# Block-sparse attention with a gated feed-forward: the first batch's attention over all keys with a per-key bias, the other three sparse, loads and groups reordered

## The chip, the cores and the metric

The kernel runs on one core of one Trainium2 chip. Five engines work from queues of their own, each in the order in which the program gave it its instructions: TensorE (PE in the profile, with its weight loads as PEld), VectorE (DVE), ScalarE (ACT), GpSimd (POOL) and SyncE (SP). SP only starts transfers here, POOL starts transfers and computes, and 16 DMA engines carry all transfers. The metric is the device time of one execution in microseconds (us); lower is better.

## The reference

There are 4 batches, 8 heads, 768 positions, head size 64. The positions form 24 blocks of 32. A query block meets its own block and the two beside it, the first and the last block, and three sampled blocks; the first and the last query block meet all keys. Behind it stand a root-mean-square norm and a gated feed-forward of width 1536 (FFN below), in float32 with bfloat16 inside the kernel.

```python
scores = scale * np.matmul(q, k.transpose(0, 1, 3, 2))
mask = np.abs(blk_i - blk_j) <= window
mask = mask | (blk_i == 0) | (blk_j == 0) | (blk_i == n_blocks - 1) | (blk_j == n_blocks - 1)
for qb in range(n_blocks):
    for kb in sampled_blocks[qb]:
        mask[qb * block:(qb + 1) * block, kb * block:(kb + 1) * block] = True
scores = np.where(mask, scores, -1000000000.0)
attn = np.exp(scores - np.max(scores, axis=-1, keepdims=True))
attn = attn / (np.sum(attn, axis=-1, keepdims=True) + 1e-09)
x = np.matmul(attn, v).transpose(0, 2, 1, 3).reshape(B * S, H * D)
xn = x / np.sqrt(np.mean(x * x, axis=-1, keepdims=True) + 1e-06) * rms_g
g = xn @ w_gate
out = (g * (1.0 / (1.0 + np.exp(-g))) * (xn @ w_val)) @ w_out
```

## The kernel before, in words

**Chunks and steps.** A chunk is 128 queries, four query blocks, of one batch. Each batch has six: five of neighbouring blocks, and one "wide" chunk of the blocks 0, 23, 1, 22 (chunks 5, 11, 17 and 22 of the 24). The outer loop (L581) has a step for each chunk and one more; a step has 10 positions, step 6 has 20. The loop only sets the order in which instructions are given to the queues: jobs are attached to a position by `do(n, ...)`, and after each position `position()` adds pieces of FFN work (L506).

**Attention of chunk i.** The keys that each query block meets are gathered into `kg`: DVE copies the neighbouring blocks and the first and last (`gather_k`, L298, L302), ACT or POOL copies the sampled ones, one block and sample at a time, at an address from a register (`sampled_k`, L310). `by_act` (L225) says which engine: ACT for two samples of three, and for all three in the first two chunks of each batch. The registers are filled from the table `kofs` (L185) by loads on ACT or POOL (`addresses`, L235). DVE copies the queries into `Qd` (`gather_q`, L325, L327). `scores` (L355) makes tiles of 8 products 128x64, 4 tiles in a sparse chunk and 8 in a wide one, and ACT takes the exponential of each tile into `ex` (L361). Two tiles `st` have room in PSUM. The values are fetched row by row: `table` (L261) writes the batch's values as bfloat16 to the DRAM tile `vtab`, and POOL starts an indirect transfer for each query block (`gather_v`, L335) with the row numbers `vidx` (L193 to L218). Step i+1 begins with `values(i)` (L376), 64 products 128x66 (128 in a wide chunk), and DVE divides by the sums into `stage` (L397, L398). Then come the squares on ACT (L405), the power on POOL (L409, L410), the product `xs` on DVE, and the turn of `xs` into `xg`: by PE (L430) for chunks 0 to 3 and the last group, by a DMA transpose started by SP (L424) for the others.

**FFN.** Chunks form groups, `sizes = [2, 2, 2, 3, 4, 4, 4, 3]`. A group's pieces are 12 gate and 12 value pieces (L445, L456: four products each, 128 columns per chunk; tanh on ACT at L449, two products on DVE at L460 and L464) and then four down pieces per chunk (L474, three products 128x512 each). `entry` (L560) gives the position from which a group's pieces are laid in, evenly until the next group's entry: in steps 3, 5, 6 (position 10), 10, 14, 18 and 22. The last group stands alone at the end. All FFN tiles and transposes share four PSUM tiles (`ps_f`).

**Before the loop.** SP loads the values of batch 0 (`load_v`), POOL the keys and 32 of each 128 query rows (`load_turned`, which also casts), PE turns the keys and those queries (`turn`, `turn_first_queries`), DVE and ACT copy them out. `keep_busy` is products that nobody reads. Weights are loaded by POOL, half of them from `W_AT` in steps 0 to 2. Batch 1 is loaded in steps 3 and 4, and batches 2 and 3 in the first four steps of the batch before them (POOL for keys and queries, SP for values). `gains` (L543) loads the norm's gain through SP, and DVE scales it, in step 3.

**Queues.** POOL's transfers use eight completion semaphores in turn, so each waits until the eighth before it has landed.

Of the kernel before, what the change touches and what calls it, by code (L numbers as in the profile page):

```python
# [18 lines left out]
def kernel(  # L19
# [18 lines left out]
    P = 128  # L38
# [36 lines left out]
    sizes = [2, 2, 2, 3, 4, 4, 4, 3]  # L75
# [64 lines left out]
    vtab = [dram.tile([NT + HB, 2 * HV], BF16, name=f"vtab{i}") for i in range(B)]  # L140

    NS = NRND * HB
    samp_i = const.tile([NS, NB * NRND * 2], I32, name="samp_i")
# [11 lines left out]
    def iota(t, lo, hi, cols, step, base):  # L155
        nc.gpsimd.iota(t[lo:hi, cols], pattern=[[step, cols.stop - cols.start]], base=base,
                       channel_multiplier=1)

    p_i = const.tile([NS, 1], I32, name="p_i")
    qb_i = const.tile([NS, NB], I32, name="qb_i")  # L160
    vidx = const.tile([P, NB], I32, name="vidx")
    every = slice(0, NB)
    nc.gpsimd.iota(p_i, pattern=[[0, 1]], base=0, channel_multiplier=1)
    nc.gpsimd.iota(qb_i, pattern=[[1, NB]], base=0, channel_multiplier=0)
    for pr in range(NP):
        load_turned(0, pr, 0)
    ident32 = const.tile([P, P], FP32, name="ident32")
    make_identity(nc, ident32)
    iota(vidx, F0 - HB, W0, every, 0, -HB)
# [5 lines left out]
    for pr in range(NP):  # L175
        load_turned(0, pr, 1, (0, QR))
    idle = const.tile([P, 2 * HV], BF16, name="idle")
    nc.vector.memset(idle, 0.0)
    for i in range(2):
        nc.vector.memset(Qd[i], 0.0)  # L180
    for i in range(2):
        nc.vector.memset(Vs[i][:, :, :, D:VW], 1.0)
    samp = samp_i.rearrange("p (a r w) -> p a r w", r=NRND, w=2)[:, :, :, 0]
    kofs = const.tile([1, NB * NRND], I32, name="kofs")
    nc.vector.tensor_scalar(out=kofs.rearrange("p (r a) -> p a r", r=NRND), in0=samp[0:1],  # L185
                            scalar1=float(HB), scalar2=None, op0=ALU.mult)
    ident = const.tile([P, P], BF16, name="ident")
    nc.vector.tensor_copy(out=ident, in_=ident32)
    qb = const.tile([NS, NB], FP32, name="qb")
    nc.vector.tensor_copy(out=qb, in_=qb_i)  # L190
    pp_i = const.tile([NS, 1], I32, name="pp_i")
    pp = const.tile([NS, 1], FP32, name="pp")
    nc.vector.tensor_scalar(out=pp_i, in0=p_i, scalar1=HB - 1, scalar2=None, op0=ALU.bitwise_and)  # L193
    nc.vector.tensor_scalar(out=pp, in0=pp_i, scalar1=float(NT), scalar2=None, op0=ALU.add)
    rb = const.tile([NS, NB, NRND], FP32, name="rb")
    good = const.tile([NS, NB, NRND], FP32, name="good")
    tmp = const.tile([NS, NB, NRND], FP32, name="tmp")
    nc.vector.tensor_copy(out=rb, in_=samp)

    nc.vector.tensor_tensor(out=tmp, in0=rb, in1=qb.unsqueeze(2).to_broadcast([NS, NB, NRND]),  # L200
                            op=ALU.subtract)
    nc.vector.tensor_tensor(out=tmp, in0=tmp, in1=tmp, op=ALU.mult)
    nc.vector.tensor_scalar(out=good, in0=tmp, scalar1=1.5, scalar2=None, op0=ALU.is_ge)
    nc.vector.scalar_tensor_tensor(out=tmp, in0=rb, scalar=1.0 - NB, in1=rb, op0=ALU.add,
                                   op1=ALU.mult)
    nc.vector.scalar_tensor_tensor(out=good, in0=tmp, scalar=-0.5, in1=good, op0=ALU.is_le,
                                   op1=ALU.mult)
    for step in range(1, NRND):
        n = NRND - step
        nc.vector.tensor_tensor(out=tmp[:, :, 0:n], in0=rb[:, :, step:], in1=rb[:, :, 0:n],  # L210
                                op=ALU.not_equal)
        nc.vector.tensor_tensor(out=good[:, :, step:], in0=good[:, :, step:], in1=tmp[:, :, 0:n],
                                op=ALU.mult)
    nc.vector.scalar_tensor_tensor(out=tmp, in0=rb, scalar=-float(NB), in1=good, op0=ALU.add,
                                   op1=ALU.mult)
    for r, lo, hi in ((1, 0, 2 * HB), (0, 0, HB), (2, 2 * HB, 3 * HB)):
        nc.vector.tensor_scalar(out=vidx[lo:hi], in0=tmp[lo:hi, :, r], scalar1=float(HB),
                                scalar2=pp[lo:hi], op0=ALU.mult, op1=ALU.add)  # L218
# [6 lines left out]
    def by_act(c, r):  # L225
        return r + 1 < NRND or c in chunks[0][1] or c in chunks[1][1]
# [15 lines left out]
    addresses(0, ET.Activation)  # L242
    addresses(1, ET.Activation)
# [3 lines left out]

    zero_rows(0)
    mhalf = const.tile([P, 1], FP32, name="mhalf")
    nc.vector.memset(mhalf, -0.5)  # L250
    eps = const.tile([P, 1], FP32, name="eps")
    nc.vector.memset(eps, DM * 1e-6)
    gain = const.tile([P, DM], FP32, name="gain")
    rmsg = const.tile([P, NP], FP32, name="rmsg")
# [6 lines left out]
    def table(b):  # L261
        if b:
            zero_rows(b)
# [13 lines left out]
    def turn_first_queries(copy):  # L277
# [246 lines left out]
    for pr in range(NP):  # L524
        cast_v(0, pr, dve)
# [168 lines left out]
```

## Time and profile before

| | us |
|---|---|
| median of 3 runs | 358.10 (353.57, 358.10, 360.46) |
| profiled execution | 354.41, of which span 352.6 |
| busy in the span: PE, DVE, ACT, POOL | 285.6, 208.1, 193.0, 156.3 |
| first scores (L355) of chunk 0 start | 18.22 |
| `stage` (L398) of chunk 0 and chunk 5 starts | 27.54, 95.41 |
| `values` of chunks 0 to 4 follow at (DVE L397 or PE L376) | 25.9, 37.6, 43.9, 60.4, 81.1 |
| POOL: 88 indirect transfers (L335), 998 ns each | 87.8 |
| ACT: 112 exponentials (L361), 606 ns each | 65.8 |
| ACT: 208 sampled key copies (L310) | 55.4 |

The start of DVE's reciprocal (L397) marks the end of a chunk's attention. From chunk 5 on these are at 95.1, 114.5, 123.6, 137.3, 145.7, 162.5 (chunk 10), 174.1, 182.8, 195.8, 210.4, 224.2 (chunk 15), 234.3, 246.0, 256.9, 267.5, 276.3 (chunk 20), 284.6, 301.9 and 316.4. In the timeline an entry such as "x8" merges instructions of one form that follow one another; the time is that of all of them, and the bracket behind it is the idle time before it and what ended it. The ends of products are modelled, so the distance from start to start tells more of PE's pace than the length.

### The profile page before, as it was taken

Reading aid. Unit: us, or ns where it says so; the run is one execution under the profiler, and the core shown is the slowest. Engines: PE = TensorE matmul, PEld = TensorE weight load, DVE = VectorE, ACT = ScalarE, POOL = GpSimd, SP = SyncE. Lnnn points to the kernel's source line nnn. Section 1 sums busy time; section 2 is a strip of 40 time slices with the busy share of each in tenths; the row PEclk is TensorE's granted clock in tenths of the full one; section 3 lists DMA queues with packets and bytes.
Section 4 is the critical chain, followed back from the end, with each engine's and each line's share of the span. In section 5 each row is a group of like instructions: output and inputs, shape, how many; then the busy total and the mean of one; then the engine's idle time right before and its main releaser. Section 6 shows DMA issues by size and latency. Waiting matters only on the chain.

```text
span 352.6 us, 10122 instructions
## 1 busy us (share of the span) xinstructions
PE 285.6 (81%) x4021; PEld 175.6 (50%) x4021; DVE 208.1 (59%) x483; ACT 193.0 (55%) x519; POOL 156.3 (44%) x250
## 2 busy tenths in 40 slices
PE   4734777388899758578978697989999998989995
PEld 1423566256766546245645453545455554534653
DVE  7615674444756746348763487860999456661770
ACT  0563752236379764646676557656866665513422
POOL 7188895170075584713288437333654550000000
PEclk9966588679999988969998999999999999999999
DMA  7779999997379397892579996767434661002002
GB/s 213 177 174 246 189 218 215 292 207 196 112 144 273 99 225 165 150 265 53 136 137 244 220 148 146 183 132 229 115 94 105 159 187 54 3 2 89 33 0 89
DMA packets 38903, 53.94 MB, mean 153 GB/s; under 512 B 12372, under 2 KB 29576, under 8 KB 38856
## 3 DMA queue, kind: packets, MB, share of 16 engines
q0 software_dynamic: 20544, 34.81, 45.9%
q1 hardware_dynamic: 18248, 18.46, 18.7%
q8 instruction: 31, 0.51, 0.6%
q10 hardware_dynamic: 64, 0.03, 0.2%
q14 instruction: 16, 0.13, 0.1%
HBM read 52.39 MB, written 9.67 MB: 176 GB/s over the span
## 4 chain that ended last, share of the span: by engine, by line
PE 46%; DMA 13%; POOL 11%; DVE 10%; issue 9%; ACT 8%; SPq 1%; POOLq 1%; ACTq 0%; DVEq 0%
PE yp L474 14%; PE gp L445 11%; PE vp L456 11%; POOL vg L335 6%; DMA kbf<-in_k_dram 4%; PE op L376 3%; DMA vraw<-in_v_dram 3%; PE st L355 3%; ACT ex L361 3%; DMA gain<-in_moe_rms_g_dram 3%; DVE u L460 3%; PE tqk L272 2%; DMA rmsr<-in_moe_rms_g_dram 2%; DVE stage L398 2%; ACT th L449 2%
## 5 line engine op out<-in xcount | busy, mean ns | idle before, releaser
L335 POOL DMA_INDIRECT vg<-vtab,vidx x88 | 87.8, 998 | 39.5 <-issue 19.1
L445 PE MATMUL gp<-xg,wg 128*128 128x256 bf16 (+2 forms) x384 | 82.7, 341 | 8.2 <-DVE u L460 6.2
L456 PE MATMUL vp<-xg,wv 128*128 128x256 bf16 (+2 forms) x384 | 82.9, 341 | 4.1 <-DVE u L460 2.8
L361 ACT ACTIVATE ex<-st 128x512 bf16<-128x512 f32 x112 | 65.8, 606 | 9.3 <-PE st L355 9.0
L449 ACT ACTIVATE th<-gp 128x256 bf16<-128x256 f32 (+2 forms) x96 | 47.7, 497 | 42.2 <-PE gp L445 40.9
L460 DVE SCALAR_TENSOR_TENSOR u<-th,gp 128x256 bf16<-128x256 bf16 (+2 forms) x96 | 53.1, 553 | 29.2 <-ACT th L449 27.7
L474 PE MATMUL yp<-wo,hps 128*128 128x512 bf16 (+1 forms) x300 | 68.2, 375 | 0.0
L464 DVE TENSOR_TENSOR hps<-u,vp 128x256 bf16<-128x256 bf16 (+2 forms) x96 | 53.3, 555 | 11.4 <-PE vp L456 1.4
L310 ACT COPY kg<-KT 128x128 bf16 x208 | 55.4, 313 | 3.1 <-issue 3.1
L409 POOL TENSOR_TENSOR ssq<-ssq,eps 128x1 f32<-128x1 f32 x24 | 4.8, 200 | 106.4 <-ACT junk L405 100.9
L445 PEld LDWEIGHTS <-wg 128*128 128x128 bf16 x384 | 36.4, 103 | 29.8 <-issue 9.6
L456 PEld LDWEIGHTS <-wv 128*128 128x128 bf16 x384 | 37.1, 103 | 27.2 <-issue 4.1
L355 PE MATMUL st<-Qd,kg 128*128 128x64 bf16 x704 | 43.8, 203 | 8.2 <-ACT ex L361 4.3
L355 PEld LDWEIGHTS <-kg 128*128 128x128 bf16 x704 | 36.8, 105 | 24.2 <-issue 9.6
L405 ACT ACTIVATE junk<-stage 128x512 bf16<-128x512 bf16 x24 | 15.1, 630 | 52.6 <-DVE stage L398 52.6
L474 PEld LDWEIGHTS <-hps 128*128 128x128 bf16 x300 | 28.0, 99 | 26.9 <-issue 0.6
L397 DVE RECIPROCAL rz<-op 128x8 f32<-128x8 f32 x24 | 4.9, 206 | 43.8 <-PE op L376 43.8
L480 ACT ACTIVATE yo<-yp 128x512 f32<-128x512 f32 (+1 forms) x25 | 14.5, 582 | 25.7 <-PE yp L474 22.9
L325 DVE COPY Qd<-QN 64x512 bf16<-64x512 bf16 x80 | 24.5, 306 | 1.2 <-ACT QN L274 0.2
L376 PEld LDWEIGHTS <-ex 128*32 128x32 bf16 x1792 | 18.9, 98 | 12.3 <-issue 12.0
L376 PE MATMUL op<-vg,ex 128*32 128x66 bf16 x1408 | 21.5, 202 | 3.8 <-DMA vg<-vtab,vidx 3.7
L258 DVE CAST Vs<-vraw 128x768 bf16<-128x768 f32 x16 | 8.8, 566 | 22.8 <-DMA vraw<-in_v_dram 22.8
(68 smaller groups left out, 243.9 us busy)
## 6 DMA issues: line engine op xcount, KB each, us to landing
vraw<-in_v_dram SPq DMA_DIRECT2D x16, 384.0 KB, 5.9
out_dram<-yo SPq DMA_DIRECT2D x19, 256.0 KB, 3.9
vtab<-Vs SPq DMA_DIRECT2D x4, 792.0 KB, 4.0
kbf<-in_k_dram POOLq DMA_DIRECT2D x16, 192.0 KB, 6.9
qbf<-in_q_dram POOLq DMA_DIRECT2D x12, 192.0 KB, 6.7
wo<-in_moe_w_out_dram POOLq DMA_DIRECT2D x2, 768.0 KB, 18.9
vg<-vtab,vidx POOLq DMA_INDIRECT x88, 4.2
out_dram<-yo SPq DMA_DIRECT2D x16, 64.0 KB, 2.6
```

Source lines behind the costliest of these rows:

```text
L310: copy(out=kgs[i % 2][:, :, j, R0 + r * HB:R0 + (r + 1) * HB], in_=KT[b % 2][:, :, bass.ds(kat[(qbs[j], r)], HB)])
L325: copy(out=to, in_=rows[:, :, qbs[0] * HB:(qbs[0] + QB) * HB])
L335: nc.gpsimd.indirect_dma_start(vgs[i % 3][:, j, :], None, vtab[b][:], bass.IndirectOffsetOnAxis(ap=vidx[:, qbs[j]:qbs[j] + 1], axis=0))
L355: nc.tensor.matmul(out=st[:, at:at + UN], lhsT=lhsT, rhs=Qd[i % 2][:, h, :, :, j * HB:(j + 1) * HB].rearrange("p a w s -> p (a w) s"), sta ...
L361: nc.scalar.activation(out=ex.rearrange("p (u s w) -> p u s w", s=HB, w=2), in_=st.rearrange("p (u w s) -> p u s w", s=HB, w=2), func=AF.E ...
L376: nc.tensor.matmul(out=op[j * BLK:(j + 1) * BLK, h // 4, at:at + VW], lhsT=lhsT, rhs=rhs, start=(n == 0), stop=(n == of - 1))
L445: nc.tensor.matmul(out=gp[:, 0:tg], lhsT=wg[:, c, f * P:(f + 1) * P], rhs=xg[:, c, 0:tg], start=(c == 0), stop=(c == KD - 1))
L449: nc.scalar.activation(out=th[:, 0:tg], in_=gp[:, 0:tg], func=AF.Tanh, scale=0.5)
L456: nc.tensor.matmul(out=vp[:, 0:tg], lhsT=wv[:, c, f * P:(f + 1) * P], rhs=xg[:, c, 0:tg], start=(c == 0), stop=(c == KD - 1))
L460: nc.vector.scalar_tensor_tensor(out=u[:, 0:tg], in0=th[:, 0:tg], scalar=1.0, in1=gp[:, 0:tg], op0=ALU.add, op1=ALU.mult)
L464: nc.vector.tensor_tensor(out=hps[f][:, 0:tg], in0=u[:, 0:tg], in1=vp[:, 0:tg], op=ALU.mult)
L474: nc.tensor.matmul(out=yp, lhsT=hps[f][:, tt * P:(tt + 1) * P], rhs=wo[:, f, lo:hi], start=(f == 0), stop=(f == NF - 1))
```

## The change

Batch 0's attention no longer selects keys. Each tile of scores holds all 8 heads for one query block and 128 keys (every third of half the positions; `all_scores`, 12 tiles a chunk), and the exponential adds a bias for each key (a partition) from the table `hide`: 0 where the query block meets the key's block, -30000 elsewhere. `all_values` multiplies with the values as they stand in SBUF, in three parts of 64 products. Batch 0 has no `vtab`, no indirect transfers, no `kg` and no sampled copies. `hide` is made by DVE ahead of `kofs`. Steps 0 to 5 have 12 positions, a tile in each; the squares of batch 0 are taken by DVE. Chunks 2 and 3 turn `xs` by DMA. In the batches 1 to 3 `by_act` leaves every third sample to POOL. Batch 0's values are loaded by POOL behind keys and queries, `samp_i` and the gain by SP; batch 1's loads stay in steps 3 and 4. The groups become `[2, 2, 2, 4, 4, 4, 4, 2]`, entering at step 2 (position 8), 4 (10), 6 (10), 11, 15, 19 and 23.

```diff
-    sizes = [2, 2, 2, 3, 4, 4, 4, 3]
+    sizes = [2, 2, 2, 4, 4, 4, 4, 2]
...
-        nc.sync.dma_start(
+        (nc.sync if b else nc.gpsimd).dma_start(
             out=t, in_=v[b, 2 * pr:2 * pr + 2].rearrange("e (p c) d -> p e c d", p=P))
...
-    nc.scalar.dma_start(out=samp_i, in_=s32.to_broadcast([NS, NB * NRND * 2]))
-    for pr in range(NP):
-        load_v(0, pr)
+    nc.sync.dma_start(out=samp_i, in_=s32.to_broadcast([P, NB * NRND * 2]))
...
+    for pr in range(NP):
+        load_turned(0, pr, 1, (0, 2 * QR))
...
     for pr in range(NP):
-        load_turned(0, pr, 1, (0, QR))
+        load_v(0, pr)
...
+    nc.vector.tensor_tensor(out=hide, in0=keys(kb), in1=queries(qb), op=ALU.subtract)
+    nc.vector.tensor_tensor(out=hide, in0=hide, in1=hide, op=ALU.mult)
+    nc.vector.scalar_tensor_tensor(out=hide, in0=hide, scalar=1.5, in1=keys(inner), op0=ALU.is_ge,
+                                   op1=ALU.mult)
...
+    for r in range(NRND):
+        nc.vector.tensor_tensor(out=far, in0=keys(kb), in1=queries(rb[:, :, r]), op=ALU.not_equal)
+        nc.vector.tensor_tensor(out=hide, in0=hide, in1=far, op=ALU.mult)
     nc.vector.tensor_scalar(out=kofs.rearrange("p (r a) -> p a r", r=NRND), in0=samp[0:1],
                             scalar1=float(HB), scalar2=None, op0=ALU.mult)
...
-        return r + 1 < NRND or c in chunks[0][1] or c in chunks[1][1]
+        return r + 1 < NRND
...
-    addresses(0, ET.Activation)
-    addresses(1, ET.Activation)
+    for i in range(PB):
+        addresses(i, ET.Pool)
+    for i in range(2):
+        addresses(i, ET.Activation)
...
+    def all_scores(i, cc, j):
+        st = ps_s.tile([P, H, UN], FP32, name="st", tag="st")
+        for h in range(H):
+            nc.tensor.matmul(
+                out=st[:, h, :], lhsT=KT[0][:, h, cc::HC],
+                rhs=Qd[i % 2][:, h, :, :, j * HB:(j + 1) * HB].rearrange("p a w s -> p (a w) s"),
+                start=True, stop=True)
+        c = chunks[i][1][j]
+        ex = exs[(i, cc, j)] = work.tile([P, 512], BF16, name="ex", tag="ex", bufs=10)
+        nc.scalar.activation(
+            out=ex.rearrange("p (u s w) -> p u s w", s=HB, w=2),
+            in_=st.rearrange("p h (u w s) -> p (h u) s w", s=HB, w=2), func=AF.Exp, scale=SCALE,
+            bias=hide[:, cc, c:c + 1])
+    def all_values(i, cc):
+        if cc == 0:
+            ops[i] = ps_o.tile([P, 2, 512], FP32, name="op", tag="op")
+        for h in range(H):
+            at = (h % 4) * VW
+            for w in range(2):
+                for j in range(QB):
+                    ex = exs[(i, cc, j)].rearrange("p (h w s) -> p h w s", h=H, w=2)
+                    nc.tensor.matmul(
+                        out=ops[i][j * BLK:(j + 1) * BLK, h // 4, at:at + VW], lhsT=ex[:, h, w, :],
+                        rhs=Vs[0][:, 2 * cc + w, h, :], start=(h % 4 == cc + w == 0),
+                        stop=(h % 4 == 3 and cc == HC - 1 and w == 1))
...
+            nc.vector.tensor_tensor_reduce(
+                out=junk, in0=stages[i], in1=stages[i], scale=1.0, scalar=0.0, op0=ALU.mult,
+                op1=ALU.add, accum_out=ssqs[i])
...
-        if i >= 4 and i not in groups[-1]:
+        if i >= 2 and i not in groups[-1]:
...
+        if m[-1] < PB:
+            step, pos = m[-1] + 1, 8 + 2 * (m[0] > 0)
...
+            for cc in range(HC):
+                for j in range(QB):
+                    do(cc * QB + j, lambda cc=cc, j=j: all_scores(i, cc, j))
+            do(7, lambda: all_values(i, 0))
+            do(11, lambda: all_values(i, 1))
...
+            if i + 2 < PB:
+                do(10, lambda: addresses(i + 2, ET.Activation))
```

The last part of a chunk's values, `all_values(i - 1, 2)`, stands at position 1 of the next step, before that position's tile.

More of the change, by code (lines that the diff above doesn't have):

```diff
@@ L197 @@
     tmp = const.tile([NS, NB, NRND], FP32, name="tmp")
[L198 to L215, printed above, removed]
@@ L359, in scores @@
                 at += UN
-        ex = exs[(i, part)] = work.tile([P, 512], BF16, name="ex", tag="ex", bufs=9)
+        ex = exs[(i, part)] = work.tile([P, 512], BF16, name="ex", tag="ex", bufs=10)
         nc.scalar.activation(
```

213 lines of the change are left out of this document (125 added, 88 removed).

## The prediction

> **What bounds the kernel now.** I read the windows of the stages first: start, batch 0 (to chunk 5's `stage`), steps 6 to 10, 11 to 14, 15 to 18, 19 to 22, and the rest. Columns: length, busy us of PE, PEld, DVE, ACT, POOL, PE's granted clock, DMA share, GB/s.
>
> ```profile
> 0.00:18.20 18.20, 10.49 (x69) 5.17 (x70) 12.73 (x41) 5.06 (x12) 8.31 (x24) 1.00 0.75 189
> 18.20:95.00 76.80, 52.30 (x896) 39.08 (x895) 39.62 (x101) 36.10 (x107) 43.64 (x65) 0.76 0.95 209
> 95.00:162.50 67.50, 52.58 (x803) 36.84 (x795) 38.58 (x101) 44.83 (x123) 36.77 (x55) 0.90 0.76 179
> 162.50:210.40 47.90, 39.68 (x643) 23.57 (x640) 30.42 (x68) 31.14 (x87) 27.32 (x42) 0.96 0.78 163
> 210.40:256.90 46.50, 42.20 (x650) 23.40 (x649) 30.90 (x69) 31.26 (x84) 20.53 (x30) 1.00 0.65 162
> 256.90:301.90 45.00, 42.77 (x639) 22.84 (x638) 30.75 (x65) 27.95 (x74) 18.24 (x31) 1.00 0.42 112
> 301.90:352.60 50.70, 45.59 (x340) 24.71 (x338) 25.09 (x44) 16.60 (x33) 1.49 (x4) 1.00 0.12 38
> ```
>
> Batch 0 takes 77 us in which no engine is busy for more than 52; the DMA share is 0.95 and PE's clock 0.76. From step 15 on PE sets the pace. The chain of waits names what batch 0 waits for (start, length, what):
>
> ```profile
> 16.57 1.17 POOL vg L335
> ...
> 20.58 5.30 DMA vg<-vtab,vidx
> ...
> 55.73 10.32 DMA gain<-in_moe_rms_g_dram
> ```
>
> The tile view of `kofs` and the timeline of ACT show what comes before ACT's first copy:
>
> ```profile
> L235 ACTq TENSOR_LOAD <-kofs x16: 275/906/1107, 4.6 to 57.5; - x16
> ...
> 10.70 1.28 ACT L274 ACT_TABLE_LOAD   x1 [10.70 <-DVE rmsg L523]
> 11.99 0.80 ACT L274 COPY KT<-tqk 128x768 bf16<-128x768 bf16 x1
> ```
>
> Six register loads begin at 4.6, when `kofs` is there, and the table load follows at 10.70: 1.01 us each. The timeline also gives the price of a tile, on a fast and on a slow PE:
>
> ```profile
> 83.81 1.07 ACT L361 ACTIVATE ex<-st 128x512 bf16<-128x512 f32 x2
> ...
> 67.70 0.63 PE L355 MATMUL st<-Qd,kg 128*128 128x64 bf16 x8
> 68.14 1.04 PE L456 MATMUL vp<-xg,wv 128*128 128x256 bf16 x4
> ```
>
> Two exponentials with nothing between end 1.07 after the first began, so the second began 0.47 after it. Eight score products take 0.44 here (67.70 to 68.14); at full clock 0.23 (two such sets, 82.19 to 82.42 to 82.66).
>
> **The change, part by part.** The profiled run (354.4) is the second fastest of four executions whose mean is 356.6; I add differences in the span to that mean.
>
> *What goes.* 22 indirect transfers (POOL 22 x 1.3 with their gaps, 29 us; 22 x 270 KB, from the tile's shape, 5.9 MB) and `vtab` (0.8 MB), of 16.1 MB moved at 209 GB/s in 76.8 us; 52 sampled copies on ACT (0.266 each, 13.8 us), 14 on POOL, the DVE copies for `kg`. The gain's wait goes too: its load stood in SP's queue behind value loads that wait for DVE, now nothing is ahead of it, and PE's 4.6 us of idleness at 66.9 with it. So batch 0 is no longer held by transfers; next is the trio PE, ACT, DVE.
>
> *Start: later by 3.7.* `kofs` is now made after the 3x24 table: DVE has the identity at 5.16+0.26 as before, then some 23 small operations at the 0.15 to 0.25 of their kind, 4.4 us, so `kofs` ends at 9.85 instead of 4.6. ACT waits for it: four loads, 4.1, and the table load, 1.28, put its first copy at 15.3 instead of 11.99. Behind that copy stand PE's third and fourth key turn (PSUM tiles), the queries, `Qd` and the first scores: 6.2 us in the profile, and up to 1.7 more if PE, idle for over 4 us by then, is at half clock (six turns take 0.82 instead of 0.49). 21.5 to 23.2; I take 21.9. The earlier keys gain nothing, ACT isn't there to copy them. POOL has seven such loads, 6.7 us; the second half of the queries and the first weights queue behind them to about 22 to 25. That costs nothing while chunk 0's first third (to about 30) covers it, up to 5 us else.
>
> *Steps 0 to 2: 32.4.* A dense chunk has 12 tiles and 192 value products. With two PSUM tiles a pair costs an exponential (0.60), eight products and their latency (0.39), two semaphores: 1.07, 0.54 a tile (exponentials at 85.03 and 86.12 had this); at half clock 1.34, 0.67. Each third of the values is 0.63 at full clock (64 products, 113.92 to 114.55), 1.2 at half (37.59 to 38.79), 0.4 and 0.9 of which ACT can't cover. 7.7 or 10.7 a step. Two register loads between tiles 10 and 11 (1.94) add about 1.2; in the steps 0 and 1 24 query transposes (0.75), in 1 and 2 PE's wait for `xs` (division, squares, power, `xs`: 0.9+0.8+0.8+0.35, against four tiles) about 0.7; step 2 has four pieces. 11.5 (mostly slow) + 10.4 + 10.5.
>
> Here a rule bears. The row: from 66.89 to 74.7 PE's products ran at the slow price for 8 us, though no gap was over 0.92. The Trainium skill (TensorE: Matmul & The Clock Gate, Part 1: The HAM clock gate) says that one busy window of about 3.4 us restores full rate; by it step 0 would be some 2 us cheaper. The trace speaks against so quick a return under gaps, so I stay with the row.
>
> *Steps 3 to 5: 42.8 with the last third.* PE per step: dense attention 12 x 0.23 + 192 x 0.011 = 4.9; a two-chunk piece is 0.437, a down piece 0.65. Laid out evenly they hold 15 pieces (6.6), 7 and 8 down (8.2), 16 (7.0): 11.5, 13.1, 11.9, sum 36.5. DVE has 7 to 8 pairs at 0.86 (91.10 to 91.96), division 0.9, `Qd` 1.3 to 1.9, `xs` 0.75, squares, in step 5 four casts (2.2): 10.4, 7.6, 11.9. The squares are an operation the trace hasn't: between 0.35 (tensor-scalar, 128x512) and 1.32 (a product plus ACT's squares); 0.8, nearest to the 0.69 of a product. Before, step 5 took 12.4 (81.1 to 93.5) for PE work of 9.5 and DVE work of 11. I take 1.1 times PE: 40.2, plus 0.5 for the edge chunk's loads (0.28 each), 1.0 for the DMA turn of chunk 3 (4.7 to land, four positions before it is read), 1.1 for the last third. Bounds 1.03 and 1.3.
>
> Chunk 5's `stage` then begins at 21.9 + 32.4 + 42.8 = 97.1, against 95.4: +1.7.
>
> *Behind batch 0: -0.6.* Steps 6 to 10 hold 30.2 us of FFN before and 23.4 after (4 pieces were done earlier; the rest moves to later groups). PE was busy 52.6 of 67.5 there, with waits for `kbf` of 2.1 and 5.7; I credit 4.0 of 6.8, bounds 1 and 6.8. Steps 11 to 14: 26.0 becomes 31.0, and 8.2 idle take 3.5 of it: +1.5. Steps 15 to 18: 31.0 both. Steps 19 to 24 and the tail: 76.9 becomes 77.7, and a two-chunk pair alone paces at 0.96 (88.62 to 89.58) instead of 0.87, 12 times: +0.8 + 1.1 = +1.9. The 24 copies that go from ACT to POOL (6.8 us there) are covered by POOL's idle third; were POOL's queue the bound in those steps, 2 to 4 more.
>
> Sum: +1.7 - 4.0 + 1.5 + 1.9 = +1.1, 356.6 + 1.1 = **358 us** (357.7): no change. A measurement here tells 2%, 7 us, from nothing; the runs shown differ by as much.
>
> **Rivals.** *PE runs free (27%).* The dense steps give PE unbroken work, the clock stays full, and the loads' wait hides: first scores 21.5, steps 0 to 2 at 8.9, 3 to 5 at 1.03 times PE plus 1.1, `stage` 5 at 87, -8.4 instead of +1.7; steps 6 to 10 give 6 instead of 4. 357.7 - 10.1 - 2 = 346. For it: steps 18 to 21 took 38.6 for PE work of 38.3. Against: these had four-chunk pieces, with more slack per wait.
>
> *Queues in order couple (29%), slower.* Each dense tile waits for an exponential that stands in ACT's queue behind tanh, and each piece's PSUM for DVE, which also holds the division, `Qd` and casts. The old step 5 paid 1.3 times PE for that. At 1.3 the steps 3 to 5 take 0.2 x 36.5 = 7.3 more, and step 6, coupled in the same way, gives one less: 366. It decides from there on, that is when their 36 exponentials are over 47.5 / 36 = 1.32 apart. Against it: that step had DVE work above PE's.
>
> *The order doesn't hold.* If the gain or weights still come late, `u` (L460) would wait for DMA in step 2 or 3; the removed 6.7 MB speak against it, and it is inside the slower case.
>
> **How the numbers follow.** 44% for no change, its own range 351 to 365; 27% for faster, around 346; 29% for slower, around 366. The start has 1.7 us of doubt, steps 0 to 2 six, steps 3 to 5 ten, the rest four either way. Leaving a tenth out on each side: 345 to 368. Faster by over 2% means below 351, slower above 365.
>
> **What would show it.** First scores at 21 to 23, ACT's first copy at 15; first weights landed by 35; the exponentials of chunk 0 0.55 to 0.7 apart; `stage` of chunk 0 near 34, of chunk 5 near 97; no wait for `vg` or gain before it; then 63 us to chunk 10's reciprocal instead of 67. If `stage` 5 begins before 90, I overpriced the coupling; after 103, underpriced it.

## The result, and the profile after

The changed kernel takes 370.66 us (median of four: 368.68, 370.40, 370.93, 377.50), the kernel before 355.84 beside it: ratio 1.042, 95% interval 1.029 to 1.056, slower. The prediction was 358, its range ended at 368. The profiled execution took 370.93, of which the span is 369.2, 16.6 more than before (352.6). Ratios use undisturbed executions alone, and two of the profiled executions below were disturbed and slower than their kernels' medians: the spread loads' (370.81) and, in the fourth set, that of all four edits (359.88).

The windows of the stages, with the columns of the prediction's first view (start; batch 0; steps 6 to 10; 11 to 14; 15 to 18; 19 to 22; the rest):

```profile
0.00:18.58 18.58, 11.03 (x89) 5.91 (x90) 8.39 (x33) 3.49 (x4) 11.51 (x30) 0.94 0.74 167
18.58:109.05 90.47, 73.21 (x1990) 61.65 (x1992) 48.89 (x128) 54.18 (x97) 16.72 (x28) 0.77 0.67 114
109.05:167.90 58.85, 43.47 (x726) 31.53 (x727) 34.48 (x91) 39.76 (x106) 40.77 (x67) 0.88 0.81 188
167.90:220.40 52.50, 44.60 (x640) 25.04 (x648) 30.83 (x66) 30.85 (x80) 27.71 (x45) 0.90 0.59 145
220.40:260.60 40.20, 35.11 (x516) 19.78 (x524) 27.62 (x57) 24.10 (x59) 18.30 (x30) 0.96 0.65 167
260.60:303.50 42.90, 39.52 (x520) 20.65 (x530) 29.36 (x62) 25.20 (x68) 21.02 (x36) 0.96 0.45 118
303.50:369.20 65.70, 59.49 (x594) 35.05 (x600) 32.33 (x64) 26.85 (x60) 5.60 (x9) 1.00 0.20 59
```

The start costs next to nothing (first scores at 18.58, before 18.22). Batch 0 takes 90.5 us instead of 77. The transfers are down as the change says (DMA share 0.67 instead of 0.95, POOL's busy time 16.7), but PE has 1990 products where it had 896, and 17.3 us without work. The chain of waits between 38 and 125 (start, length, what) shows where most of them lie:

```profile
41.38 1.63 issue
...
46.05 2.88 issue
...
54.87 0.54 issue
...
72.55 4.23 issue
...
84.14 7.33 DMA xg<-xs
...
113.55 7.30 DMA xg<-xs
```

"issue" is time for which the profile shows no wait. The four pieces in batch 0 are 9.3 of the 17.3 us. The timeline of PE tells what they are (start, length, products, and in the bracket the idle time before them):

```profile
71.95 0.61 PE L431 MATMUL op<-Vs,ex 128*32 128x66 bf16 x54
76.78 0.27 PE L431 MATMUL op<-Vs,ex 128*32 128x66 bf16 x10 [4.23 <-issue]
...
91.51 1.01 PE L524 MATMUL gp<-xg,wg 128*128 128x256 bf16 x4 [2.73 <-DMA xg<-xs]
```

A third of a chunk's values is 64 products that need the same four `ex` tiles and the same `Vs` from the first to the last. PE does 54 of them, stands still for 4.23 us, and does the other ten. No semaphore can be late in the middle of such a set. In this time, 72.5 to 76.8, PE is busy for 0.07 us, DVE for 0.34, ACT and POOL for nothing, and the DMA share is 0.38. The stalls at 41.4, 46.1 and 54.9 are of the same kind: in the middle of a set of values, or of a score tile. The profile of the kernel before has no such stall. Of the other 8 us without work, 2.7 are the wait for `xg` in the last line; the rest are waits for ACT's `ex` and DVE's `xs` and `u`.

What is left is that PE had no instructions. The page counts the transfers that bring them (queue, kind: packets, MB, share of 16 engines), in the kernel before and now:

```profile
q8 instruction: 31, 0.51, 0.6%
q8 instruction: 40, 0.66, 0.8%
```

Each packet is 16,384 bytes. They are PE's: the kernel before has 4021 products with a weight load each, 8042 instructions for 31 packets, and the changed one 5109 weight loads and as many products (36 of these are missing from the trace), 10218 for 40: some 256 to a packet both times. Before chunk 5's reciprocal 6 packets start in the kernel before and 16 now. The times of these packets in the trace, beside the stalls of at least 0.5 us in the middle of a set (us):

```
kernel            stall from   to     packet starts  takes  ends    stall ends after that
changed              41.38   43.01       40.58       0.96   41.54   1.47
                     46.05   48.93       46.63       0.89   47.53   1.40
                     54.86   55.40       53.00       0.89   53.90   1.50
                     72.55   76.78       73.82       1.67   75.49   1.29
xs turned by PE      41.18   44.12       41.92       0.96   42.89   1.23
                     91.91   93.19       90.95       0.95   91.90   1.29
later weights        66.59   69.24       66.86       0.93   67.79   1.45
```

In the changed kernel, its repeat and the five kernels of the experiments below that have such stalls in batch 0 there are 26 of them. Each ends 1.2 to 1.6 us after the end of a packet of 16,384 bytes. The 4.23 us are thus made of 1.27 until the fetch begins, 1.67 for the fetch, and 1.29 behind it.

The places of the stalls say the same. These are the windows from the start of the span to the start of each stall in the changed kernel, with the columns as above; the first bracket counts PE's products:

```profile
0.00:41.40 41.40, 30.43 (x607) 22.68 (x607) 23.05 (x69) 18.22 (x27) 18.62 (x40) 0.70 0.84 149
0.00:46.06 46.06, 33.47 (x735) 25.29 (x735) 23.63 (x71) 19.61 (x30) 18.62 (x40) 0.68 0.88 155
0.00:54.88 54.88, 38.73 (x863) 29.94 (x863) 27.53 (x80) 24.60 (x37) 20.24 (x43) 0.66 0.87 151
0.00:72.56 72.56, 54.91 (x1375) 44.09 (x1375) 38.77 (x111) 37.89 (x63) 23.86 (x49) 0.74 0.78 136
```

From 607 to 735 to 863 it is 128 products each time, to 1375 four times 128; 128 products and their weight loads are 256 instructions, one packet. All 26 stalls begin after product 351, 607, 735, 863, 1247, 1375 or 1631, and all these lie a multiple of 128 apart. PE stands still exactly where a packet's instructions are used up.

### The profile page after: what moved, and what is told of

It is laid out like the page before. It is cut to its first block, busy times and chain, and to the rows that moved or that the text cites. A ratio compares the mean times of both kernels' runs of the same rounds, so it can differ in the third digit from the quotient of the medians.

```text
span 369.2 us, 12171 instructions
## 1 busy us (share of the span) xinstructions
PE 306.4 (83%) x5073; PEld 199.6 (54%) x5109; DVE 211.9 (57%) x498; ACT 204.4 (55%) x473; POOL 141.6 (38%) x243
## 4 chain that ended last, share of the span: by engine, by line
PE 45%; issue 18%; POOL 13%; ACT 8%; DVE 7%; DMA 6%; ACTq 2%; POOLq 0%; SPq 0%; DVEq 0%
PE vp L535 11%; PE gp L524 11%; PE yp L553 9%; POOL vg L375 6%; PE st L409 5%; DMA xg<-xs 4%; PE op L431 3%; ACT ex L401 2%; PE st L395 2%; ACT ex L415 2%; POOL kg L350 2%; PE op L447 2%; DMA kbf<-in_k_dram 2%; POOL kbf L106 2%; ACTq L280 2%
## 5 line engine op out<-in xcount | busy, mean ns | idle before, releaser
L524 PE MATMUL gp<-xg,wg 128*128 128x256 bf16 (+1 forms) x368 | 80.5, 336 | 14.1 <-DMA xg<-xs 7.7
L535 PE MATMUL vp<-xg,wv 128*128 128x256 bf16 (+1 forms) x379 | 84.0, 347 | 5.7 <-DVE u L539 5.3
L539 DVE SCALAR_TENSOR_TENSOR u<-th,gp 128x256 bf16<-128x256 bf16 (+1 forms) x96 | 53.0, 552 | 49.4 <-ACT th L528 47.0
L375 POOL DMA_INDIRECT vg<-vtab,vidx x66 | 66.7, 1010 | 17.2 <-issue 17.0
L528 ACT ACTIVATE th<-gp 128x256 bf16<-128x256 f32 (+1 forms) x96 | 47.3, 493 | 44.0 <-PE gp L524 41.2
L415 ACT ACTIVATE ex<-st,hide 128x512 bf16<-128x512 f32 x72 | 47.6, 687 | 29.4 <-PE st L409 27.0
L543 DVE TENSOR_TENSOR hps<-u,vp 128x256 bf16<-128x256 bf16 (+1 forms) x96 | 53.2, 554 | 14.1 <-PE vp L535 4.9
L409 PE MATMUL st<-Qd,KT 128*128 128x64 bf16 x576 | 34.6, 216 | 9.3 <-DVE Qd L365 3.7
L409 PEld LDWEIGHTS <-KT 128*128 128x128 bf16 x576 | 30.7, 116 | 14.2 <-issue 9.3
L350 ACT COPY kg<-KT 128x128 bf16 x132 | 36.3, 312 | 0.0
## 6 DMA issues: line engine op xcount, KB each, us to landing
out_dram<-yo SPq DMA_DIRECT2D x19, 256.0 KB, 3.9
```

The costliest lines, as they stand in the source:

```text
L350: copy(out=kgs[i % 2][:, :, j, R0 + r * HB:R0 + (r + 1) * HB], in_=KT[b % 2][:, :, bass.ds(kat[(qbs[j], r)], HB)])
L375: nc.gpsimd.indirect_dma_start(vgs[i % 3][:, j, :], None, vtab[b][:], bass.IndirectOffsetOnAxis(ap=vidx[:, qbs[j]:qbs[j] + 1], axis=0))
L409: nc.tensor.matmul(out=st[:, h, :], lhsT=KT[0][:, h, cc::HC], rhs=Qd[i % 2][:, h, :, :, j * HB:(j + 1) * HB].rearrange("p a w s -> p (a w) ...
L415: nc.scalar.activation(out=ex.rearrange("p (u s w) -> p u s w", s=HB, w=2), in_=st.rearrange("p h (u w s) -> p (h u) s w", s=HB, w=2), fun ...
L524: nc.tensor.matmul(out=gp[:, 0:tg], lhsT=wg[:, c, f * P:(f + 1) * P], rhs=xg[:, c, 0:tg], start=(c == 0), stop=(c == KD - 1))
L528: nc.scalar.activation(out=th[:, 0:tg], in_=gp[:, 0:tg], func=AF.Tanh, scale=0.5)
```

## The experiments

The theories when the experiments were written. A: PE uses up its instructions faster than they arrive among the loads, and the DMA turns of `xs` stand behind the same loads. B: the exponentials, dearer with a bias, and the two score tiles (`st`) set the pace. C: the regrouping of the batches 1 to 3 costs the loss. D and E divide A: is it the number of instructions, or the loads? Within a set the kernels ran on one chip; the first and the fifth set ran on the same one, each other set on another. Times are medians, ratios (with their intervals) are to the kernel before on the same chip, "stage n" is the start of chunk n's reciprocal in the profiled execution.

### First set (the kernel before: 355.2)

**Batch 1's loads spread.** Of the two pairs at position 4 of the steps 3 and 4, one transfer group every four to six positions:

```diff
-            if i in (3, 4):
-                for pr in range(2 * (i - 3), 2 * (i - 3) + 2):
-                    do(4, lambda pr=pr: load_v(1, pr))
-                    do(4, lambda pr=pr: load_kq(1, pr))
+            for pr, at, vat in zip(range(NP), ((4, 6), (4, 10), (5, 2), (5, 6)), ((3, 2), (3, 8), (4, 2), (4, 8))):
+                if i == vat[0]:
+                    do(vat[1], lambda pr=pr: load_v(1, pr))
+                if i == at[0]:
+                    do(at[1], lambda pr=pr: load_kq(1, pr))
```

> The changed kernel, with batch 1's loads spread: the values one pair of heads at a time from step 3 position 2 to step 4 position 8, keys and queries from step 4 position 4 to step 5 position 6, instead of two pairs at once at position 4 of steps 3 and 4. Theory A (PE runs out of instructions while their fetch stands among the loads, and the DMA turn of xs stands behind them too): the 4.23 us in the middle of a values part at 72.55 falls below 1, the 2.73 before the second group's first product below 1, chunk 5's stage starts at 102 to 105 instead of 109.05, time 363 to 367. Theory B (the dense steps are slow because the exponential with a bias and the two score tiles pace them): stage 5 stays within 2 us of 109, time 369 to 372.

Measured: 367.04, ratio 1.029 (1.020 to 1.037). Stage 5 at 102.7. The stall near 72 fell to 1.58 and the wait for `xg` to 1.27, both above the bound of 1; those at 41 and 46, where batch 1 isn't loading yet, stayed (1.93, 3.17), and one of 1.02 came at 29.8. The products are the same and stage 5 is 6 us earlier, so B doesn't explain these 6 us. The median fell by 3.6 us only.

**`xs` of chunks 2 to 5 turned by PE:**

```diff
-        if i >= 2 and i not in groups[-1]:
+        if i >= PB and i not in groups[-1]:
```

> The changed kernel, with the xs of chunks 2 to 5 turned by PE instead of by a DMA transpose. Theory A: the two waits for xg at the second and third group's entry (2.73 and some 4.1) go; 16 turns on PE (0.51 for four warm, 2.0 in all) and their copies are added; the instruction stalls (1.63, 2.88, 4.23) stay; stage 5 at 106 to 107, time 365 to 368. Theory B: PE and DVE are the pace, so the added turns cost and the waits come back elsewhere: 370 to 373.

Measured: 371.55, ratio 1.046 (1.037 to 1.055). The waits for `xg` went, but stage 5 came at 110.3: the stall at 41 grew to 2.94, and the one near 72 became three (1.31, 1.34, and 1.28 at 92), with 16 more turns to fetch. The time expected (365 to 368) didn't come. This wait is a place where time shows, not one where it can be saved alone.

**No bias in batch 0's exponentials:**

```diff
-            in_=st.rearrange("p h (u w s) -> p (h u) s w", s=HB, w=2), func=AF.Exp, scale=SCALE,
-            bias=hide[:, cc, c:c + 1])
+            in_=st.rearrange("p h (u w s) -> p (h u) s w", s=HB, w=2), func=AF.Exp, scale=SCALE)
```

> The changed kernel without the bias in batch 0's exponentials, so that the mask of batch 0 is left out; everything else as it was. Theory B: the exponential falls from 0.687 to 0.606, two in a row start 0.47 apart instead of 0.58, and with 72 of them in the path 5 to 8 us go: stage 5 at 101 to 104, time 363 to 366. Theory A: PE at half clock, its instruction stalls and the waits for xg set the pace, the exponentials have slack: stage 5 at 107 to 109, time 368 to 371.

This kernel leaves batch 0's mask out. Measured: 371.86, ratio 1.038 (1.030 to 1.047); stage 5 at 110.2. The group of the exponentials in the changed kernel (busy us, mean ns; then idle us before them and what ended most of it):

```profile
L415 ACT ACTIVATE ex<-st,hide 128x512 bf16<-128x512 f32 x72 | 47.6, 687 | 29.4 <-PE st L409 27.0
```

and in this one:

```profile
L415 ACT ACTIVATE ex<-st 128x512 bf16<-128x512 f32 x72 | 41.5, 596 | 35.3 <-PE st L409 32.2
```

The bias costs 91 ns each, 6.1 us of ACT, and leaving it out adds 5.9 us to ACT's idleness. ACT waits for PE's scores far more than PE for ACT. B falls as to the bias; what the two score tiles cost is seen in the third set.

**Groups and `by_act` of before,** batch 0 dense:

```diff
-    sizes = [2, 2, 2, 4, 4, 4, 4, 2]
+    sizes = [2, 2, 2, 3, 4, 4, 4, 3]
...
-        return r + 1 < NRND
+        return r + 1 < NRND or c in chunks[0][1] or c in chunks[1][1]
```

> The changed kernel with the group sizes of before (2, 2, 2, 3, 4, 4, 4, 3) and by_act of before (ACT copies all three samples in the first two chunks of a batch); batch 0 dense as changed. Theory A: stage 5 stays at 109, the part behind it falls from 260.2 to the 257.2 of before, time 367 to 369. Theory C (the regrouping costs most of the loss): the part behind falls to 250 or less, time 358 to 362.

Measured: 373.90, ratio 1.054 (1.045 to 1.062). Stage 5 at 109.6 and 260.8 from there to the end, with the new groups 260.4. C falls as to the time: the new groups save 7 us up to chunk 10 (59.1 instead of 66.0) and give them back from chunk 14 on (148.8 instead of 142.6). A's own figures missed here: it had expected 257.2 behind stage 5 and 367 to 369 in all. `by_act` puts more register loads on ACT before its first copy (16.95 instead of 15.03), and the first scores start 2.1 later (20.71).

### Second set (the kernel before: 355.9)

**Four query blocks' values in one product.** The four exponentials of a third of the keys write into one tile, so that 128 weight columns lie side by side (two tiles of four parts, also for the sparse chunks, in place of ten single ones):

```diff
-        ex = exs[(i, cc, j)] = work.tile([P, 512], BF16, name="ex", tag="ex", bufs=10)
+        if j == 0:
+            exs[(i, cc)] = work.tile([P, 2 * H, QB, BLK], BF16, name="ex4", tag="ex4", bufs=2)
...
-            out=ex.rearrange("p (u s w) -> p u s w", s=HB, w=2),
+            out=exs[(i, cc)][:, :, j, :].rearrange("p u (s w) -> p u s w", w=2),
...
-                for j in range(QB):
-                    ex = exs[(i, cc, j)].rearrange("p (h w s) -> p h w s", h=H, w=2)
-                    nc.tensor.matmul(
-                        out=ops[i][j * BLK:(j + 1) * BLK, h // 4, at:at + VW], lhsT=ex[:, h, w, :],
+                nc.tensor.matmul(
+                    out=ops[i][:, h // 4, at:at + VW],
+                    lhsT=exs[(i, cc)][:, 2 * h + w].rearrange("p j s -> p (j s)"),
```

> The changed kernel with the values of four query blocks in one product: 16 products 128x66 on 128 weight columns for each third, instead of 64 on 32 columns; 48 instead of 192 in a dense chunk, 144 products instead of 288. The exponentials write into one tile for four parts, two such tiles instead of ten single ones. Theory A (PE uses up its instructions faster than they are fetched among the loads): no stall in the middle of a set above 1 us, 8.5 us less; a third of the values at the price of the score products (0.029 each warm, 0.058 cold), 0.46 to 0.93 instead of 0.69 to 1.07; stage 5 at 97 to 101 instead of 109, time 358 to 363. Theory D (the stalls come from late transfers alone, whatever the number of instructions): they stay at 1.6 to 4.2 near 41, 46 and 72, stage 5 at 106 to 109, time 367 to 371.

Measured: 360.49, ratio 1.011 (1.004 to 1.018). No stall in the middle of a set of 0.5 us or more is left in batch 0. The timeline of PE in step 1, where the changed kernel stood still at 41.4 and 46.1:

```profile
38.73 1.03 PE L412 MATMUL st<-Qd,KT 128*128 128x64 bf16 x16
39.58 1.07 PE L433 MATMUL op<-Vs,ex 128*128 128x66 bf16 x16
40.46 0.62 PE L412 MATMUL st<-Qd,KT 128*128 128x64 bf16 x8
42.09 1.06 PE L433 MATMUL op<-Vs,ex 128*128 128x66 bf16 x16 [1.02 <-ACT ex L419]
42.96 1.04 PE L412 MATMUL st<-Qd,KT 128*128 128x64 bf16 x16
44.36 1.16 PE L412 MATMUL st<-Qd,KT 128*128 128x64 bf16 x16 [0.35 <-ACT ex L419]
47.17 0.61 PE L512 MATMUL tx<-ident,xs 128*128 128x128 bf16 x4 [1.65 <-DVE xs L508]
```

Sixteen products there take 0.88 from start to start (39.58 to 40.46), 64 took 1.0 (44.33 to 45.33): a set on a cold PE (granted clock 0.50) is cheaper by 0.12 only. Stage 5 came at 99.8 instead of 108.8. These 9.0 us are close to the sum of the four stalls (1.63 + 2.88 + 0.54 + 4.23 = 9.28), but they are not the stalls alone: up to there PE is busy for 67.7 us instead of 73.2 and without work for 13.5 instead of 17.3, so part is less work on PE, and other waits (for `ex` and `xs`, as above) have grown where the stalls were. What the run shows is that the stalls go: with 1127 products instead of 1990 in this stretch, and 33 packets instead of 40 in the whole run, under the same loads. D falls.

**Weights loaded later,** so that the steps 1 and 2 have few transfers and the steps 3 and 4 more:

```diff
             if i == 1:
-                do(3, lambda: load_w(wg, moe_w_gate, 6, NF))
-                do(3, lambda: load_w(wv, moe_w_val, 6, NF))
-                do(8, lambda: load_wo(0, NF // 2))
+                pass
             if i == 2:
-                do(4, lambda: load_wo(NF // 2, NF))
+                do(2, lambda: load_w(wg, moe_w_gate, 6, NF))
+                do(2, lambda: load_w(wv, moe_w_val, 6, NF))
                 do(4, gains)
+                do(9, lambda: load_wo(0, NF // 2))
+                do(9, lambda: load_wo(NF // 2, NF))
```

> The changed kernel with the last half of the gate and value weights loaded in step 2 position 2 (instead of step 1 position 3) and the down weights in step 2 position 9 (instead of step 1 position 8 and step 2 position 4). Theory A with the loads as the cause of the late fetch: the stalls near 41.4 (1.63) and 46 (2.88) go, the stage of chunk 2 starts at 57 to 59 instead of 61.2; the weights then stand with batch 1's loads, and the stall near 72 stays or grows; time 367 to 372. Theory E (PE runs dry by its own pace whatever the loads): both early stalls stay within 0.7 of their size, stage of chunk 2 at 61.

Measured: 371.53, ratio 1.045 (1.038 to 1.053). The stalls near 41 and 46 are gone, stage 2 came at 57.5 instead of 61.2; new ones stand where the loads now are:

```profile
69.24 1.01 PE L431 MATMUL op<-Vs,ex 128*32 128x66 bf16 x58 [2.65 <-issue]
74.33 0.27 PE L431 MATMUL op<-Vs,ex 128*32 128x66 bf16 x10 [1.42 <-issue]
```

The products are the same as in the changed kernel, only the transfers have moved. E falls: it takes both, the many instructions and the loads. In the 3 us before each of the changed kernel's four stalls the DMA share is 1.10 to 1.20 (packets overlap, so it can pass 1). The two runs together, fewer products under the same loads and the same products under moved loads, show A. The second also prices it: 5.05 us of stalls left the steps 0 to 2, and stage 2 came 3.75 earlier.

**Both, wide products and spread loads** (the two edits above):

> Both edits: the values of four query blocks in one product, and batch 1's loads spread. Theory A: no instruction stall and no wait for xg above 1.3 in batch 0; stage 5 at 93 to 98, time 353 to 360, as fast as the kernel before or faster. If the part behind batch 0 takes the gain back (its loads are started by the same steps, so they should move with it): 362 to 366.

Measured: 357.40, ratio 1.006 (1.001 to 1.011). Stage 5 at 94.3, 259.3 behind it, the wait for `xg` 0.94.

**The kernel before with the gain loaded early:**

```diff
-        nc.sync.dma_start(out=gain, in_=moe_rms_g.unsqueeze(0).to_broadcast([P, DM]))
+        if not scaled:
+            nc.sync.dma_start(out=gain, in_=moe_rms_g.unsqueeze(0).to_broadcast([P, DM]))
+            return
...
+        if i == 1:
+            do(9, lambda: gains(0))
         if i == 3:
-            do(9, gains)
+            do(9, lambda: gains(1))
```

> The kernel before with the gain's load started in step 1 position 9, ahead of batch 1's value loads in SP's queue, instead of step 3 position 9; its scaling stays where it was. It measures what the change's better place for the gain is worth by itself. If the wait of 10.32 us in the chain was PE's only idleness there (4.6 us at 66.9), 3 to 5 us go: ratio 0.986 to 0.992. If the wait only covers another (xs, or the weights), within 1 us of before.

Measured: 353.87, ratio 0.993 (0.989 to 0.998), 2 us. Stage 3 came at 64.0 instead of 67.3, but stage 5 at 94.5 instead of 95.2: in the chain the wait for the gain (10.32) gave way to one for the down weights `wo` (17.42 from 49.50). Behind a wait for one load stood the next. So the early gain by itself is worth 2 us, between the two answers.

### Third set (the kernel before: 371.2)

Built on wide products and spread loads.

**Six score tiles in the steps 0 to 2:**

```diff
-        st = ps_s.tile([P, H, UN], FP32, name="st", tag="st")
+        more = i < 2 and (cc * QB + j) % 3 or i == 2 and cc < 2 and j % 2
+        st = (ps_f if more else ps_s).tile([P, H, UN], FP32, name="st", tag="ff" if more else "st")
```

> The kernel with values of four query blocks in one product and spread loads, and besides two of three score tiles of chunks 0 and 1 (every second of the first eight of chunk 2) in the four PSUM tiles of the FFN, which has no work there: six score tiles instead of two. It asks what still holds the steps 0 to 2 at 11.7, 11.8 and 14.2 us. If it is the turn of the two tiles between PE and ACT, with PE at half clock: PE gets up to five tiles ahead, ACT's 12 exponentials (0.58 apart, 7.0) and two register loads (1.9) become the pace, 9 to 10 a step, stage 5 at 88 to 91 instead of 94.3, time 351 to 355. If PE's own work at half clock holds them (12 x 0.48 and 48 products at 0.058, 8.5, and the turns): less than 1 us a step, 355 to 358.

**Register loads later:**

```diff
-    for i in range(2):
-        addresses(i, ET.Activation)
...
-            if i + 2 < PB:
-                do(10, lambda: addresses(i + 2, ET.Activation))
+            if i in (3, 4):
+                for c in range(3):
+                    do(2 + 4 * c, lambda c=c: addresses(3 * (i - 3) + c, ET.Activation))
```

> The kernel with values of four query blocks in one product and spread loads, and ACT's register loads moved from before its first key copy (9.7 to 13.7) and from between the tiles 10 and 11 of the steps 0 to 3 into the steps 3 and 4 (positions 2, 6, 10). If ACT's place in the queue holds the first copy, as the prediction had it: the first scores at 15.5 to 17 instead of 18.6, the 1.3 us of idle ACT at tile 10 gone, stage 2 at 51 to 54 instead of 56.3, time 352 to 355. If keys or queries landing hold the start: first scores at 18 or later, time 355 to 358.

**All four edits:**

> All four edits together: values of four query blocks in one product, spread loads, six score tiles in the steps 0 to 2, ACT's register loads in the steps 3 and 4. Where both are held by what they remove: stage 5 at 84 to 88, time 346 to 352, faster than the kernel before by 1 to 2.5%. If transfers (weights, batch 0's second query half) then hold the start: 353 to 357.

Measured: six tiles 360.58, ratio 0.975 (0.969 to 0.981); later register loads 357.22, 0.966 (0.960 to 0.973); all four 355.22, 0.960 (0.954 to 0.965). The times are longer than expected where the edits work (351 to 355, 352 to 355, 346 to 352), and yet the ratios are better than was expected, because this chip runs the kernel before in 371 us; wide products and spread loads alone did not run on it, so the times don't price the single edits. By the stages: six tiles make step 1 shorter by 1.0 (10.8 instead of 11.8), on the bound between the two answers, and stage 5 comes at 91.4 instead of the 94.3 of the second set. So the two score tiles do cost, some 3 us by these two profiles on two chips: B was right to that extent. Without the register loads the first scores start at 16.44 and stage 2 at 51.3, as expected, stage 5 at 92.0; with both it is 89.5 (84 to 88 was expected).

### Fourth and fifth set

**The kernels again, side by side,** where the kernel before took 373.0 (fourth) and 355.7 (fifth):

> The kernel before, once more with a profile, beside the three below on the same chip. In the third set its median was 371.2 instead of 355 to 356. If the chip of this set is like the first two: 353 to 358, no instruction stall. If it is like the third: 367 to 373, and by theory A (fetch among transfers) its profile shows idle PE put down to nothing in the middle of value sets, in batch 0's gathers, as the third set's kernels show it in chunk 6.

> The changed kernel, once more with a profile. On a chip like the first two: 369 to 372, ratio 1.04, stalls of 1.6, 2.9 and 4.2 at the places known. On a chip like the third, theory A says that its stalls are no shorter there: 372 to 385.

> Values of four query blocks in one product, and spread loads, beside the others: 355 to 358 on a chip like the second set's (ratio 1.00 to 1.01), 361 to 365 on one like the third's, where the six tiles alone came to 360.6.

> All four edits together, beside the kernel before on this chip: on a chip like the first two, stage 5 at 88 to 90 and chunk 6 done 16 to 17 later, time 348 to 353, ratio 0.98 to 0.99. If its gain in the third set was that chip's alone: 355 to 358, ratio 1.00.

> All four edits together once more, to see them beside the kernel before on another chip. On a chip where the kernel before takes 353 to 358: time 348 to 355, ratio 0.98 to 1.00, because there the kernel before has no instruction stalls to lose and the edits gain 3 to 5 us over the wide products and spread loads (357.4). On one where it takes 368 to 375: 353 to 358, ratio 0.95 to 0.96, as in the third and fourth set.

The last one adds to the four edits:

```diff
-        if i >= 2 and i not in groups[-1]:
+        if i >= 2 and i not in groups[-1] and i not in (3, 5):
```

> All four edits, and besides the xs of chunks 3 and 5 (the last of the second and third group) turned by PE instead of by a DMA transpose. The waits for xg at the second group's entry (1.3 to 1.9) and at the third's go, eight turns (1 us) come: 0 to 3 us less than the four edits alone. Turning all of chunks 2 to 5 by PE in the changed kernel brought nothing (371.6); if it is the same here: within 1 us.

| | us | ratio (interval) | stage 5 | from there to the end |
|---|---|---|---|---|
| fourth: before, again | 374.15 | 1.002 (0.996 to 1.009) | 101.2 | 271.2 |
| changed, again | 377.88 | 1.013 (0.999 to 1.028) | 108.4 | 265.9 |
| wide, spread | 362.74 | 0.975 (0.966 to 0.984) | 95.1 | 267.5 |
| all four edits | 356.13 | 0.954 (0.946 to 0.963) | 88.9 | 269.1 |
| fifth: all four edits | 349.44 | 0.983 (0.974 to 0.993) | 89.5 | 256.0 |
| all four, chunks 3, 5 by PE | 350.17 | 0.989 (0.984 to 0.994) | 88.8 | 260.0 |

All four edits together beat the kernel before on the three chips on which they ran, by 1.7 to 4.6%, and each interval lies below 1, in the fifth set only just (0.974 to 0.993). The turns by PE bring nothing, again. On the fourth set's chip the change costs 1.3%, with an interval that holds no change. The changed kernel's batch 0 takes as long there as in the first profile, stalls and all (2.02, 3.59, 3.16), while the kernel before loses 6.0 us in batch 0 and 13.8 behind it. In batch 0 of the kernel before, PE there does four or five value products, is idle for half a microsecond, and so on; the timeline of PE:

```profile
47.82 0.29 PE L376 MATMUL op<-vg,ex 128*32 128x66 bf16 x5 [0.48 <-issue]
48.59 0.27 PE L376 MATMUL op<-vg,ex 128*32 128x66 bf16 x4 [0.48 <-issue]
49.34 0.47 PE L376 MATMUL op<-vg,ex 128*32 128x66 bf16 x18 [0.47 <-issue]
```

These pieces make 4.7 us between 22 and 50. They don't fit the 26 stalls: the idle times stand after products 361, 366 and 370, not 128 apart; a packet of instructions ended at 49.28, 0.06 before the last line and not 1.2 to 1.6; and another such row, from 28.7 to 32.4, has no packet near its end. A had expected idle time here as a sign of its own; the idle time is there, but nothing shows it to be the same shortage. Its cause, and why some chips have it, stay open.

## Why the prediction was wrong

**The step that failed** is the sum of the steps 0 to 5: 32.4 + 42.8 = 75.2 us from the first scores to chunk 5's `stage`. It took 90.5. Laid out along PE, the 15.3 us that are missing are 9.3 of stalls for instructions, 1.7 of the wait for `xg` (2.73, where 1.0 was counted), and 4.3 that are left, nearly all in the steps 0 to 2 at half clock. This says where the time lies; without the stalls not all of it would come back (5.05 gave 3.75 with the weights loaded later). The sum took PE's work as durations of products and asked of each what it waits for by semaphore. It never asked whether the instructions would be there. The figures for it were at hand: 896 products in that window before, 192 value products for each of six chunks in the prediction's own sum, and 31 packets of instructions on the page. None of the rivals held this mechanism. The prediction's own sign for a late `stage` 5 (after 103: coupling underpriced) would have led to the wrong cause.

**Start: +0.4 instead of +3.7.** ACT's first copy was at 15.03 as worked out (15.3). But 3.55 us lay behind it, not 6.2: PE had finished its turns by then, and only copies and `Qd` followed. So the term's mechanism was half right. The reading that ACT's register loads hold that copy was right: without them the first scores came at 16.44.

**Steps 0 to 2: 41.4 instead of 32.4** (18.58 to 60.0). 5.05 of the 9.0 are the stalls. The rest, 4, is put to the half clock: the granted clock was 0.50 in the whole window from 19.2 to 52, where the prediction had one step "mostly slow" and two faster ones. No run changes the clock alone, so this share is argued and not shown. Here the row was right against the rule that was weighed. The windows of a stretch in which PE never paused (length, busy PE, PEld, DVE, ACT, POOL, clock, DMA share, GB/s):

```profile
22.70:26.00 3.30, 3.30 (x106) 2.92 (x106) 2.95 (x14) 2.36 (x5) 0.00 (x0) 0.50 1.16 168
26.00:29.20 3.20, 3.20 (x112) 2.78 (x108) 2.79 (x8) 1.36 (x4) 0.00 (x0) 0.50 1.29 198
```

For 6.5 us PE was busy without a gap, by the profile's modelled ends, and the granted clock stayed at 0.50. The Trainium skill (TensorE: Matmul & The Clock Gate, Part 1: The HAM clock gate) would have it at full rate after one busy window of about 3.4 us; this trace does not agree.

**Steps 3 to 5: 49.0 instead of 42.8.** The stall (4.23) and the wait for `xg` beyond what was counted (1.7) are 5.9 of the 6.2. With these taken off, the factor of 1.1 for FFN and dense attention side by side comes out as assumed, and so does the price of DVE's squares (0.77 with their read-out, 0.8 assumed). The bias was not priced at all. It costs 91 ns an exponential, and the kernel without it was no faster.

**Behind batch 0: +2.9 instead of -0.6.** Steps 6 to 10 gained 8.3 (59.1 instead of 67.4), twice the credit, and the later groups gave it back. With the groups of before this part is as long (260.8), so the regrouping is neutral in this pair of profiles. There the wait for batch 3's keys (`kbf`) between the reciprocals of chunks 12 and 13 is 6.4 us instead of 3.2, about the difference. That stretch took 17.3 us there, 13.0 in the kernel before, and 11.5 in the same kernel with the gain loaded early. So this wait alone can make 3 us between one kernel and the next. It doesn't clear the change, though: behind stage 5, seven of the eight profiles of the changed kernel and its variants up to the second set take 259.3 to 262.3 and the eighth 266.4, the kernel before 257.5 in both of its profiles up to there. Whether these 3 us belong to the change stays open.

**The rivals.** "Queues in order couple" gave 366, the nearest number, but by another mechanism, so its nearness is luck: ACT waited 27 us for PE's scores, and the exponentials without a bias changed nothing. "PE runs free" named what would have come without the stalls, though not so fast: with wide products and spread loads chunk 5's reciprocal came at 94.3, not 87. What was right is that the gathers and the gain's wait go: neither stands in batch 0's chain now.

## What to carry to other kernels

Where a change trades transfers for many small products, count the instructions against the time as well as their durations: here 1990 products (and as many weight loads) in 90 us starved PE where loads held the DMA share above 1, 1127 in 81 us under the same loads did not, and one product with 128 weight columns in place of four with 32 ended the stalls. An idle engine in the middle of a set that needs nothing new has no wait to look for; look at the packets of its instructions, and count whether the stalls lie a whole number of packets apart. And judge a ratio of some per cent on more than one chip: the same two kernels stood at 1.042 on one and at 1.013 on another.

## What the runs showed of the hardware

PE's instructions come in packets of 16,384 bytes, some 256 instructions each (10218 for 40 packets, 8042 for 31). A stall for instructions begins where a packet's instructions are used up, and it ends 1.2 to 1.6 us after the end of the next packet, in all 26 cases. The packet itself takes 0.9 to 1.9 us. So the late start and the time behind it make most of a stall of 3 to 4 us (2.56 of 4.23 in the longest). The exponential of 128x512 out of PSUM takes 596 ns without a bias from a column and 687 with one.
